# Order of a step's VectorE work in the attention: the next tile's maximum ahead of the older tile's mask

## The chip, the cores and the metric

One core of a Trainium2 chip runs the whole program in one launch. The metric is the device time of that core in microseconds (us). Engines are written as in the profile: PE is TensorE's matmul, PEld its weight load, DVE is VectorE, ACT ScalarE, POOL GpSimd, SP SyncE.

## The reference, cut to what matters

The program is a thresholded attention followed by two dense mixtures of experts. Only the attention is touched here.

```python
scores = scale * np.matmul(q, k.transpose(0, 1, 3, 2))        # batch 2, heads 8, 576 x 576, head size 64
thresh = np.max(scores, axis=-1, keepdims=True) - tau
scores = np.where(scores >= thresh, scores, -1000000000.0)
scores = scores - np.max(scores, axis=-1, keepdims=True)
attn = np.exp(scores)
attn = attn / (np.sum(attn, axis=-1, keepdims=True) + 1e-09)
return np.matmul(attn, v).astype(np.float32)
```

The result, 1152 tokens of 512 numbers, goes through eight experts with gates that are normalised eight times over rows and columns, and then through four experts with given weights. Each expert is `relu(x @ w1) @ w2` with 1024 hidden columns. All of it is float32; most products are made from a high and a low part of each operand.

## The kernel before, in words

The attention works on 72 tiles ("units") of 128 query rows by all 576 keys, one after the other, in a software pipeline that is written out by hand: the program order of each engine is the order of the code, and nothing moves an instruction afterwards. `Attention.step` (lines 389 to 429) issues one step. In step t it handles seven units at different ages; the names used here are those of line 394:

- `nxt` is unit t+2: PE makes its scores (`scores`, line 253) into a PSUM tile `sc`. There are two such tiles, so the scores of unit t+2 can't start before unit t's tile has been read for the last time.
- `a` is unit t+1: DVE takes the row maximum of its scores (`top`, line 275), then derives from it the bias of the exponential and the threshold (`line`, lines 279 and 280); ACT then takes the exponential (`exp`, line 284).
- `d` is unit t: DVE compares its scores with the threshold and multiplies the exponential by the result, with the row sum as a by-product (`mask`, line 288; this is the last reader of unit t's `sc`). Then come the sum's guard (`guard`, line 292) and the reciprocal (`norm`, line 296), and POOL scales the tile (line 298).
- `x` is unit t-2: PE transposes it into `et` (`turn`, lines 306 and 308); ACT copies it out as `eth` or `e` (`hi`, line 313); DVE forms the low part `etl` (`lo`, line 323).
- `c`, `z` and `y` are older units, which PE multiplies by the values (`mix`, lines 341, 348, 350), with outputs copied by ACT and DVE.

The pieces that DVE runs for `a` and `d`, and the exponential between them:

```python
def top(self, u):
    V.tensor_reduce(st[:, 0:1], u["sc"][:, :, :HS], axis=AX.XY, op=ALU.max)
def line(self, u):
    V.tensor_scalar(st[:, 1:2], st[:, 0:1], lin[:, 0:1], None, op0=ALU.mult)      # the bias
    V.tensor_scalar(st[:, 2:3], st[:, 0:1], lin[:, 1:2], None, op0=ALU.subtract)  # the threshold
def exp(self, u):
    A.activation(ex, u["sc"][:, :, :HS], AF.Exp, bias=u["st"][:, 1:2], scale=esc)
def mask(self, u):
    V.scalar_tensor_tensor(ex, u["sc"][:, :, :HS], st[:, 2:3], ex, op0=ALU.is_ge, op1=ALU.mult,
                           accum_out=st[:, 3:4])
def guard(self, u):
    V.tensor_scalar(u["st"][:, 4:5], u["st"][:, 3:4], 1e-9, None, op0=ALU.add)
def norm(self, u):
    V.reciprocal(st[:, 5:6], st[:, 4:5])                    # then POOL scales the tile
```

Within a step PE's program order is: the transposes of `x`, the older exact units' value products, `fill(0)`, the scores of `nxt`, the other value products, `fill(1)`. `fill` is expert work that has nothing to do with this tile: from step 20 on, up to three groups of 12 expert matmuls a step (lines 461 and 489) with their own ACT and DVE instructions (`hh` line 467, `hl` line 470). There is none in steps 0 to 19 and 36 to 39. Until the first expert runs, steps cut expert weights into high and low parts instead (ACT line 96, then POOL line 98 or, in even steps, DVE line 100). POOL's order within a step is: scale of `d`, the weights' low part, the low part of the next keys (`kl`, line 76) and of the next queries (`qs`, line 240). The first units' scores come straight from float32 operands (line 261), all others from split ones (line 270).

After step 76 the attention is over; the experts that are left run to the end.

Of the kernel before, what the change touches and what calls it, by code (L numbers as in the profile page):

```python
# [29 lines left out]
def attention_two_moe_kernel(ctx, tc, qP, kP, qT, kT, vp, tau, wg, w1, w1s, w2, dp, m2w1s, m2w2, out):  # L30
# [80 lines left out]
    class Attention:  # L111
# [277 lines left out]
        def step(self, fill, side):  # L389

            us, t = self.units, self.t
            un = lambda i: us[i] if 0 <= i < len(us) else None
            self.load()
            nxt, a, d, x, c, z, y = (un(t + i) for i in (2, 1, 0, -2, -3, -4, -5))
            if x:
                self.turn(x)
            if d:
                self.mask(d)
            if a:
                self.top(a)  # L400
            if d:
                self.guard(d)
            if a:
                self.line(a)
            if d:
                self.norm(d)
            for part, u in ((2, y), (1, z), (0, c)):
                for g in u["mix"] if u else ():
                    if g["head"]["exact"]:
                        self.mix(g, part)  # L410
            if x:
                self.hi(x)
            for u, late in ((z, False), (y, True)):
                for g in u["mix"] if u else ():
                    if late == (g["head"]["exact"] and g["head"]["h"] < H - 1):
                        self.out(g)
            fill(0, bool(c and c["mix"]))
            if a:
                self.exp(a)
            if x:  # L420
                self.lo(x)
            if nxt:
                self.scores(nxt)
            self.run(self.later)
            for g in c["mix"] if c else ():
                if not g["head"]["exact"]:
                    self.mix(g, 0)
            fill(1, bool(c and c["mix"] or z and z["mix"]))
            self.run(self.late)
            for w in self.work.pop(t, ()):  # L430
                w()
            side()
            self.t += 1
            return self.t < len(us) + 5
# [74 lines left out]
    with ExitStack() as att:  # L509
# [23 lines left out]
        def side():  # L533
            if at.t >= -1:
                fetch(2)
            if at.t >= nA0 - 3 and raws and room[0] and (at.t < nA1 or room[0] > 2 or at.t % 2):
                room[0] -= 1
                cook()
            if at.t == 20:
                nc.sync.dma_start(wg_sb, wg)  # L540
                nc.sync.dma_start(dp_sb, dp)
            if at.t == 24:
                split(V, V, wg2[:, :, :E1], wg2[:, :, E1:], wg_sb)
# [26 lines left out]
        def fill(phase, busy):  # L570
            if phase == 0:
                if 0 <= at.t < nA0 - 3:
                    room[0] -= 1
                    cook(None if at.t % 2 else at.later)
                spent[0] = pull(3)
            elif left[0] or not busy:
                pull(max((RA1 if at.t < nA1 + 3 else RA2) - spent[0], 0), True)
# [502 lines left out]
```

## Time and profile before

| what | value |
|---|---|
| device time, median of 3 runs (lowest to highest) | 1357.63 us (1355.26 to 1357.83) |
| the profiled execution: span from first to last instruction | 1353.7 us |
| PE busy over the span | 1320.6 us (98%) |
| PEld busy | 1181.8 us (87%) |
| DVE busy | 679.6 us (50%) |
| ACT busy | 562.3 us (42%) |
| POOL busy | 688.6 us (51%) |
| first and last mask of the attention start at | 7.93 us and 238.46 us |

The profile gives for the profiled execution its span; what lies around the span is not in it. The median of the runs is 3.9 us above the span. Shares over the whole span say little here, because the attention is its first sixth and the other five sixths are expert matmuls; the prediction reads the attention by stages.

### The profile page before, as it was taken

What the parts mean: (1) busy time and instruction counts of PE and PEld (TensorE: products, weight loads), DVE (VectorE), ACT (ScalarE), POOL (GpSimd) and SP (SyncE); (2) the same over time, 40 slices, a digit from 0 to 9 for tenths busy, and PEclk for the clock granted to TensorE, in tenths of its full rate; (3) what the DMA queues carried; (4) which work ended last, traced back from release to release, by engine and by line L of the source; (5) the groups of instructions that cost most, each with busy time, mean ns of one, the idle gap of its engine ahead of it and who ended that gap; (6) DMA issues with size and microseconds to landing.
All of it is one profiled execution on the core that took longest, in us unless ns stands there. A gap on an engine that the chain in (4) does not pass through costs nothing.

```text
span 1353.7 us, 21670 instructions
## 1 busy us (share of the span) xinstructions
PE 1320.6 (98%) x8089; PEld 1181.8 (87%) x8089; DVE 679.6 (50%) x1600; ACT 562.3 (42%) x1291; POOL 688.6 (51%) x830
## 2 busy tenths in 40 slices
PE   7998999999999999999999999999899999999998
PEld 4588999899888989899898989989789889898987
DVE  6899999365853433434343343434433434343343
ACT  6877777322542423323242332325433334242331
POOL 5866976441774345345434533544963554354330
PEclk9999999999999999999999999999999999999999
DMA  5522330100221111111011111101111101110001
GB/s 173 173 85 72 93 96 26 32 24 24 91 66 39 55 47 40 48 40 62 24 55 47 40 48 40 63 24 56 37 34 55 48 24 56 47 60 27 32 8 63
DMA packets 42058, 73.63 MB, mean 54 GB/s; under 512 B 5088, under 2 KB 10336, under 8 KB 41952
## 3 DMA queue, kind: packets, MB, share of 16 engines
q1 hardware_dynamic: 41664, 71.96, 16.8%
q8 instruction: 64, 1.05, 0.3%
q14 instruction: 42, 0.34, 0.1%
q10 hardware_dynamic: 288, 0.28, 0.1%
HBM read 69.86 MB, written 2.36 MB: 53 GB/s over the span
## 4 chain that ended last, share of the span: by engine, by line
PE 83%; DVE 8%; POOL 4%; ACT 3%; issue 2%; DMA 1%; POOLq 0%; ACTq 0%; DVEq 0%
PE mm L997 37%; PE mm L887 32%; PE mm L489 5%; PE mm L461 3%; DVE ex L288 2%; DVE st L275 1%; PE sc L270 1%; PE et L306 1%; ACT ex L284 1%; PE pv L350 1%; PE pv L341 1%; PE pv L348 1%; POOL wl L76 1%; DVE etl L323 1%; DVE xy L772 0%
## 5 line engine op out<-in xcount | busy, mean ns | idle before, releaser
L997 PE MATMUL mm<-wh,hs 128*128 128x512 f32 x1344 | 436.7, 398 | 3.7 <-DVE hs L863 3.7
L76 POOL TENSOR_TENSOR wl<-raw,wh 128x512 fp32r<-128x512 f32 x154 | 199.1, 1304 | 328.4 <-ACT wh L71 326.5
L997 PEld LDWEIGHTS mm<-wh,hs 128*128 128x128 f32 x1344 | 253.0, 188 | 66.3 <-DVE hs L863 10.1
L1005 DVE SCALAR_TENSOR_TENSOR acc<-mm,p,acc 128x512 f32<-128x512 f32 x181 | 135.9, 751 | 308.1 <-PE mm L997 308.1
L997 PE MATMUL mm<-wl,hs 128*128 128x512 f32 x672 | 264.7, 394 | 0.0
L892 ACT COPY s<-mm 128x288 f32<-128x288 f32 x84 | 33.6, 401 | 453.5 <-PE mm L887 453.5
L863 DVE SCALAR_TENSOR_TENSOR hs<-mm,hs 128x288 fp32r<-128x288 f32 x252 | 114.8, 456 | 104.0 <-ACT hs L862 103.7
L997 PEld LDWEIGHTS mm<-wl,hs 128*128 128x128 f32 x672 | 127.0, 189 | 27.3
L887 PE MATMUL mm<-xh,wl 128*128 128x288 f32 x672 | 144.3, 296 | 2.6 <-ACT w L892 1.4
L887 PE MATMUL mm<-xl,wh 128*128 128x288 f32 x672 | 143.8, 295 | 0.0
L887 PE MATMUL mm<-xh,wh 128*128 128x288 f32 x672 | 143.8, 295 | 0.0
L862 ACT ACTIVATE hs<-mm 128x288 fp32r<-128x288 f32 x252 | 104.2, 414 | 71.8 <-DVE mm L914 66.6
L76 POOL TENSOR_TENSOR wl<-ws,wh 128x512 fp32r<-128x512 f32 x88 | 114.5, 1305 | 36.6 <-ACT wh L71 26.9
L887 PEld LDWEIGHTS mm<-xh,wl 128*128 128x128 f32 x672 | 110.0, 188 | 7.3 <-ACT w L892 1.9
L887 PEld LDWEIGHTS mm<-xh,wh 128*128 128x128 f32 x672 | 108.1, 188 | 0.0
L887 PE MATMUL mm<-xth,wl 128*128 128x288 f32 x504 | 107.9, 295 | 0.0
L887 PEld LDWEIGHTS mm<-xl,wh 128*128 128x128 f32 x672 | 107.9, 188 | 0.0
L887 PE MATMUL mm<-xth,wh 128*128 128x288 f32 x504 | 107.7, 295 | 0.0
L887 PE MATMUL mm<-xtl,wh 128*128 128x288 f32 x504 | 107.7, 295 | 0.0
L869 POOL TENSOR_SCALAR ht<-hs 128x128 fp32r<-128x128 f32 x168 | 49.2, 298 | 112.9 <-ACT hs L862 97.8
L71 ACT CAST wh<-raw 128x512 fp32r<-128x512 f32 x154 | 95.7, 624 | 13.3 <-PE mm L887 10.4
L625 POOL TENSOR_TENSOR ws<-raw 128x512 f32<-128x512 f32 x44 | 57.7, 1311 | 54.6 <-DMA raw<-in_w1s 32.5
(169 smaller groups left out, 2412.0 us busy)
## 6 DMA issues: line engine op xcount, KB each, us to landing
raw<-in_w SPq DMA_DIRECT2D x88, 256.0 KB, 3.0
raw<-in_w1s SPq DMA_DIRECT2D x56, 256.0 KB, 2.8
raw<-in_m2w1s SPq DMA_DIRECT2D x32, 256.0 KB, 2.7
raw<-in_m2w SPq DMA_DIRECT2D x32, 256.0 KB, 2.8
kr<-in_kT SPq DMA_DIRECT2D x22, 288.0 KB, 2.9
vr<-in_vp SPq DMA_DIRECT2D x24, 160.0 KB, 2.3
qr<-in_qT SPq DMA_DIRECT2D x8, 288.0 KB, 2.8
out_y<-acc SPq DMA_DIRECT2D x8, 256.0 KB, 2.0
```

Of the source, the lines that this page charges most:

```text
L71: A.copy(hi, src)
L76: el.tensor_tensor(lo, src, f(hi), op=ALU.subtract)
L461: T.matmul(ph[:, :n], lhsT=a[:, kt * P:(kt + 1) * P], rhs=x[:, kt, n0:n0 + n], start=i == 0 and kt == 0, stop=i == 2 and kt == KT - 1)
L489: T.matmul(py[:, :256], lhsT=x, rhs=a[:, c0:c0 + 256], start=i == 0, stop=i == 3 * FT - 1)
L625: G.tensor_tensor(s, a, b, op=op)
L862: A.activation(hh, src, AF.Relu)
L863: V.scalar_tensor_tensor(hl, src, 0.0, f(hh), op0=ALU.max, op1=ALU.subtract)
L869: G.tensor_scalar(tail[j][:, :, q:q + 32], f(side[s][j][:, :, 2 * P:]), 1.0, 1.0, op0=ALU.mult, op1=ALU.mult)
L887: T.matmul(m, lhsT=w[:, (2 * g + kt) * P:(2 * g + kt + 1) * P], rhs=operand(u, kt, lo), start=first and j == 0, stop=j == len(ops) - 1, sk ...
L892: A.copy(z[name], m)
L997: T.matmul(py, lhsT=hs[x][:, k, o:o + P], rhs=w, start=n == 0, stop=n == 3 * HF - 1)
L1005: V.scalar_tensor_tensor(acc[t], py, s, acc[t], op0=ALU.mult, op1=ALU.add)
```

## The change

In each step DVE took the mask of unit t, the maximum of unit t+1, the guard of t, bias and threshold of t+1, the reciprocal of t. Now it takes the maximum of t+1, the mask of t, bias and threshold of t+1, then guard and reciprocal of t next to each other. No instruction is added or removed, and no other engine's order is changed.

```diff
             if x:
                 self.turn(x)
+            if a:
+                self.top(a)
             if d:
                 self.mask(d)
             if a:
-                self.top(a)
+                self.line(a)
             if d:
                 self.guard(d)
-            if a:
-                self.line(a)
-            if d:
                 self.norm(d)
```

One step of DVE in the middle of the attention, before; `etl`, `eth` and `xf` are the step's other DVE work, and the bracket names the engine whose semaphore an instruction waits for:

```order
L288 SCALAR_TENSOR_TENSOR ex,st<-sc,st,ex 128x576 [waits DVE_49,Activation_49]
L275 TENSOR_REDUCE st<-sc 128x1 [waits PE_49]
L292 TENSOR_SCALAR st<-st 128x1 [waits DVE_49]
L279 TENSOR_SCALAR st<-st,lin 128x1 [waits DVE_49]
L280 TENSOR_SCALAR st<-st,lin 128x1
L296 RECIPROCAL st<-st 128x1 [waits DVE_49]
L323 TENSOR_TENSOR etl<-et,eth 128x4x128 [waits Activation_49]
```

The same step now:

```order
L275 TENSOR_REDUCE st<-sc 128x1 [waits PE_49]
L288 SCALAR_TENSOR_TENSOR ex,st<-sc,st,ex 128x576 [waits Activation_49]
L279 TENSOR_SCALAR st<-st,lin 128x1 [waits DVE_49]
L280 TENSOR_SCALAR st<-st,lin 128x1
L292 TENSOR_SCALAR st<-st 128x1 [waits DVE_49]
L296 RECIPROCAL st<-st 128x1 [waits DVE_49]
L323 TENSOR_TENSOR etl<-et,eth 128x4x128 [waits Activation_49]
```

The maximum, which waits for PE, now stands ahead of the mask, which waits for ACT; the reciprocal follows directly on the guard, whose result it reads.

The start of the attention on PE (the scores of the first four units in float32, then the first transposes and the first split scores), which is the same before and now:

```order
L261 MATMUL sc<-kr,qr 128x288 [waits DMAHW1_49,DMAHW0_49]
L261 MATMUL sc<-kr,qr 128x288 [waits DMAHW5_49]
L261 MATMUL sc<-kr,qr 128x288 x2
L261 MATMUL sc<-kr,qr 128x288 [waits DVE_49,PE_49]
L261 MATMUL sc<-kr,qr 128x288
L261 MATMUL sc<-kr,qr 128x288 [waits DVE_49,PE_49]
L261 MATMUL sc<-kr,qr 128x288
L306 MATMUL et<-ident,ex 128x128 [waits Pool_49]
L306 MATMUL et<-ident,ex 128x128 x3
L308 MATMUL er<-ident,ex 64x128
L270 MATMUL sc<-kh,qs 128x288 [waits DVE_49,PE_49,Pool_49]
```

From the third unit on, each unit's scores wait for DVE, namely for the mask that frees their `sc` tile. PE's row is unchanged; the DVE instruction that it waits for has moved one place back.

## Rows read from the trace of the kernel before

**Rows 1.** Stages: stretch, length; busy PE, PEld, DVE, ACT, POOL; clock, DMA.

```profile
122.00:141.00 19.00, 15.09 (x104) 13.16 (x103) 17.59 (x52) 13.04 (x24) 12.09 (x18) 1.00 0.19 58
141.00:240.00 99.00, 96.93 (x763) 94.48 (x762) 92.20 (x283) 75.48 (x148) 74.84 (x104) 1.00 0.23 72
```

**Rows 2.** The chain that ended last, around 40 us: start, length, engine and line.

```profile
39.10 0.84 ACT ex L284
...
39.96 0.82 DVE ex L288 x2
```

**Rows 3.** The same chain from 62 to 240 us, shares by line.

```profile
by line: PE mm L489 13.7%; PE mm L461 10.2%; DVE ex L288 7.9%; PE sc L270 7.7%; DVE st L275 6.8%; PE et L306 6.7%; issue 6.4%; PE pv L350 4.9%; PE pv L348 4.3%; ACT ex L284 3.8%; DVE etl L323 3.1%; POOL ex L298 2.0%; PE pv L341 2.0%; DVE st
```

**Rows 4.** DVE's waits, 6 to 240 us: total us, times, longest.

```profile
DVE ex L288 <- ACT ex L284: 15.0, 31, 1.7
```

**Rows 5.** The same wait, 62 to 240 us.

```profile
DVE ex L288 <- ACT ex L284: 5.8, 19, 0.8
```

**Rows 6.** PE at the start: start, length, operation [idle before, releaser].

```profile
3.49 4.35 PE L261 MATMUL sc<-kr,qr 64*128 64x288 f32 x8 [3.49 <-DMA qr<-in_qP]
8.91 2.25 PE L261 MATMUL sc<-kr,qr 64*128 64x288 f32 x4 [1.06 <-DVE ex L288]
...
15.51 0.85 PE L270 MATMUL sc<-kh,qs 128*128 128x288 f32 x2 [0.39 <-POOL qs L240]
16.16 0.68 PE L270 MATMUL sc<-kl,qs 128*128 128x288 f32 x2
...
23.06 0.54 PE L270 MATMUL sc<-kh,qs 128*128 128x288 f32 x2 [2.38 <-POOL qs L240]
```

**Rows 7.** DVE at the start, one row of its timeline: the first mask.

```profile
7.93 0.82 DVE L288 SCALAR_TENSOR_TENSOR ex<-sc,st,ex 128x576 f32<-128x576 f32 x1 [0.84 <-ACT ex L284]
```

**Rows 8.** POOL at the start, one row of its timeline: unit 3 is scaled.

```profile
18.85 0.74 POOL L298 TENSOR_SCALAR ex<-ex,st 128x576 f32<-128x576 f32 x1 [2.55 <-DVE st L296]
```

**Rows 9.** DVE's timeline over one even step without expert work.

```profile
39.96 0.82 DVE L288 SCALAR_TENSOR_TENSOR ex<-sc,st,ex 128x576 f32<-128x576 f32 x1 [0.77 <-ACT ex L284]
...
40.70 0.75 DVE L275 TENSOR_REDUCE st<-sc 128x1 f32<-128x576 f32 x1
...
41.49 0.21 DVE L279 TENSOR_SCALAR st<-st,lin 128x1 f32<-128x1 f32 x1
...
41.74 0.15 DVE L296 RECIPROCAL st<-st 128x1 f32<-128x1 f32 x1
...
42.14 1.14 DVE L100 TENSOR_TENSOR wl<-raw,wh 128x512 fp32r<-128x512 f32 x1
43.20 0.81 DVE L288 SCALAR_TENSOR_TENSOR ex<-sc,st,ex 128x576 f32<-128x576 f32 x1
```

**Rows 10.** PE's timeline, the scores of three steps running.

```profile
38.14 0.53 PE L270 MATMUL sc<-kh,qs 128*128 128x288 f32 x2 [0.56 <-DVE ex L288]
...
41.13 0.53 PE L270 MATMUL sc<-kh,qs 128*128 128x288 f32 x2
...
44.07 0.40 PE L270 MATMUL sc<-kh,qs 128*128 128x288 f32 x1 [0.59 <-DVE ex L288]
```

**Rows 11.** First of 18 close pairs: a mask, and the scores behind it.

```profile
67.34 0.80 DVE L288 SCALAR_TENSOR_TENSOR ex<-sc,st,ex 128x576 f32<-128x576 f32 x1
...
68.29 0.37 PE L270 MATMUL sc<-kh,qs 128*128 128x288 f32 x1 [0.32 <-DVE ex L288]
```

**Rows 12.** Last of the 18 close pairs.

```profile
220.18 0.82 DVE L288 SCALAR_TENSOR_TENSOR ex<-sc,st,ex 128x576 f32<-128x576 f32 x1
...
221.56 0.30 PE L270 MATMUL sc<-kh,qz 128*128 128x288 f32 x1
```

**Rows 13.** PE's longest wait in total, 62 to 240 us.

```profile
PE et L306 <- DVE etl L323: 6.3, 9, 1.0
```

**Rows 14.** DVE before the attention: an instruction, and one reading its result.

```profile
4.39 0.15 DVE L527 TENSOR_SCALAR on<-tau_sb 128x1 f32<-128x1 f32 x1 [2.58 <-DMA tau_sb<-in_tau]
4.58 0.15 DVE L528 TENSOR_SCALAR esc<-on 128x1 f32<-128x1 f32 x1
```

## The prediction

> **What bounds the kernel now.** I read the busy times by stage first, then the chain that ended last, then the waits, then the timelines of DVE and PE side by side. The stages show that the attention has no single bound. From 141 to 240 us PE is busy 97 of 99 us, its weight loads 94 and DVE 92; in the stretch without expert work, 122 to 141 us, DVE is busy 17.6 of 19 us and PE only 15.1 [rows 1]. So DVE and PE are both nearly full and hand work to each other in every step. The reader is to see in the chain at 40 us a ring on which no engine is full: the exponential of unit t+1 on ACT (0.84 us) releases its mask on DVE, after the mask come the next maximum, guard and bias, and the bias releases the next exponential [rows 2]. One turn takes 0.86 us (39.10 to 39.96) for the exponential, 0.74 us from mask to maximum, 0.79 us from there to the bias (of it 0.12 for the guard's place, so 0.67 for the maximum), and 0.3 us from the bias to the exponential (estimated): 2.7 us. While the exponential runs, DVE stands still for 0.77 us [rows 9]. DVE waits so 31 times in the attention, 15.0 us in all [rows 4], and 19 of these times, 5.8 us, lie behind 62 us [rows 5]. The maximum could run in these gaps, and that is what the new order does.
>
> What it costs is on PE. There are two score tiles; the mask is the last reader of one, and PE can start scores 0.87 us after the start of the mask that frees their tile (43.20 to 44.07) [rows 9, 10]. The new order puts 0.67 us of maximum ahead of the mask, and the maximum itself waits for PE. So a ring that did not bind before can: scores, maximum, mask, scores.
>
> **The change, part by part.** No instruction is added or removed, and PE, ACT, POOL and SP keep their orders, so no DMA moves on its queue. Four things change.
>
> *1. The start.* The first scores are slow: units 0 and 1 end at 7.84 us (3.49 + 4.35), and unit 2 takes 2.25 us [rows 6]. Before, the first mask started at 7.93 and the scores of unit 2 followed 0.98 us later [rows 6, 7]. Now the maximum of unit 1 goes first, from 7.9 us; the mask follows at 8.55, scores 2 run from 9.5 to 11.8, maximum 2 follows, mask 1 at 12.5, scores 3 from 13.4 to 15.7, maximum 3, mask 2 at 16.4, scores 4 at 17.3 instead of 15.51, 1.33 us long (15.51 to 16.84), maximum 4 at 18.6, mask 3 at 19.3. Its reciprocal comes 1.2 us behind it (0.74 for the mask, 0.12 to 0.13 for each of two small instructions, 0.19 for the guard), and POOL can scale unit 3 at 20.7 us. Before it did so at 18.85 us, after 2.55 us of waiting for this reciprocal [rows 8]; behind it on POOL stand the weights', keys' and queries' low parts, for which PE waits at 23.06 us [rows 6]. All of that moves by 1.9 us. Bounds: 0, if other work covers it, and 3.
>
> *2. The steps without expert work, 32 to 50 us.* Two steps take 5.93 us (38.14 to 44.07) [rows 10]. The new ring for two steps: scores 0.8 (two pairs of matmuls of 0.53, which overlap), maximum 0.67, mask to reciprocal 1.18, from there through the other DVE work to the next step 1.46 (41.74 to 43.20), maximum 0.67, mask to scores 0.87 [rows 9, 10]; together 5.65 us. That is 0.28 less, three times: 0.8 us gained. Behind 50 us PE runs without a gap up to the expert work, and nothing is gained. Parts 1 and 2 give +1.1 us.
>
> *3. The steps with expert work, and 36 to 39.* I set each mask's start against that of the scores it releases. If DVE did not wait for the exponential, the mask moves by 0.67 us, and the scores can't start before 0.67 + 0.87 = 1.54 us behind the old start of the mask. From step 19 on, 18 pairs are closer than that, the first with 0.95 us [rows 11], the last with 1.38 [rows 12]; what is missing, less what DVE waited anyway, sums to 6.5 us. Not all of it is lost: nine times, 6.3 us in all, PE waits at its next transposes for DVE's `etl` [rows 13], and a late score matmul can vanish there. But PE's later end moves the transposes, ACT's copy and DVE's `etl` with it, and that has hardly any slack. I take half, 3.3 us; the ends are 0 and 6.5. Against it stands the gain from DVE's waits. On the chain between 62 and 240 us the mask has 7.9% of 178 us, or 14 us, which is 17 masks of 0.82 us out of 53 [rows 3]. A third of the 5.8 us of waits [rows 5] is thus on the path: 1.9 us gained; the ends are 0 and 5.8.
>
> *4. Guard and reciprocal side by side.* The reciprocal now waits for the instruction just ahead of it. Such a pair of small instructions starts 0.19 us apart (4.39 and 4.58) [rows 14]; in the old order two steps of the small work take 0.25 us (41.49 to 41.74), so about 0.12 each [rows 9]. That is 0.07 us a step. It counts where DVE is on the chain, in the same 17 steps: 1.2 us. The ends are 0 and 72 x 0.07 = 5.0 us. The Trainium skill (VectorE: DVE Perf Modes, "The DRAIN you can't avoid") says that chaining VectorE instructions with or without semaphores takes the same time. By that rule this part would be nothing and the forecast 1.2 us lower; the 0.19 us above speaks against it for small instructions.
>
> Sum: 1.1 + 3.3 - 1.9 + 1.2 = +3.7 us. Against the profiled execution's span of 1353.7 us that gives 1357.4 us; the median of the runs is 3.9 us above that span, which I take over: **1361.3 us**. What follows the attention is mostly PE's expert work, so I let the whole shift through.
>
> **The rivals.**
>
> *Faster: the exponential's ring decides.* If PE's close pairs vanish in its waits for `etl` and the start is covered, what is left is the gain: 0.8 us of part 2 and up to all 5.8 us of waits, less 1.2 us for the reciprocal: -5.4 us, 1352.2 us. For it: the wait recurs 31 times, and on the chain at 40 us it is what ends last [rows 2, 4]. Against it: behind 62 us the chain runs through PE for longer than through the mask, and PE has 2 us of idle time in 99 [rows 1, 3]. It decides where DVE, not PE, ends a step in more than the 17 of 53 steps. The Trainium skill's advice (Perfetto Trace Analysis, "Optimization Strategy") is to find the recurring gaps on the engine that should be full and to make what they wait for start sooner; by it this rival would be the forecast. Chance 0.2.
>
> *No change: the slack takes both.* PE's expert matmuls fill what the new order moves, the start's delay is swallowed by the later queue on POOL, and the sum stays within 0.2%, 2.7 us, which is about what a measurement of this kernel can tell from no change: 1357.6 us. For it: PE and DVE are both near full, so neither can be moved far. Chance 0.24.
>
> *Much slower: every step pays.* All close pairs count in full and every step pays the reciprocal: 1.1 + 6.5 + 5.0 = +12.6 us, 1370.2 us. It decides if PE is bound to the mask at every step. Chance 0.1, within slower.
>
> That the change does not do what it says I leave out: DVE's rows stand in the new order, and nothing reorders them.
>
> **How the numbers follow.** The forecast and the much slower case have 0.56 together, faster 0.2, no change 0.24. The range leaves out the outer part of the faster rival and the last of the much slower one: 1354.0 to 1368.5 us.
>
> **What would show it.** Right, step by step: the masks' waits for the exponential fall from 15.0 us to a few; the maximum gets a wait for PE's scores, which it hardly had, above all before 30 us; the scores of unit 6 start near 25 us instead of 23.06; two steps near 40 us take about 5.65 us; PE's waits for the mask grow behind 62 us; the last mask starts about 4 us later than at 238.46 us; guard and reciprocal stand 0.19 us apart. Wrong: the last mask earlier than before, or the start unmoved, or PE's waits for the mask unchanged while the time rises.

## The result and the profile after

The changed kernel takes **1364.38 us** (median of four runs; 1363.16 to 1366.98), the kernel before beside it 1357.63 us (median of three; a fourth run, of 2225.16 us, is far out of line and counts nowhere). The ratio on record is 1.0065, 95% interval 1.0052 to 1.0078: **8.8 us slower** (7.1 to 10.6). That is inside the range and on the side of the forecast, but 5 us more than its +3.7 us. The medians of these few runs stand only 6.7 us apart, which the ratio does not rest on alone. The clock speaks for the larger figure: three of the four changed runs had a mean granted clock of 0.997 and took 1363.16 to 1364.47 us, while 28 runs of the kernel before at 0.997, in the experiments below, have a median of 1355.8 us, some 8.5 us less.

The profiled execution took 1364.47 us, with a span of 1362.7 us against 1353.7 us: +9.0 us. In every run of the experiments the time is 1.7 to 1.9 us above the span. So the profiled execution of the kernel before took about 1355.5 us, a quick one, and of the 3.9 us that the prediction added to its span some 2 us are the difference between two runs; its shift of +3.7 us does not hang on that.

Where it arises is read from the masks, the same instruction in both traces. The table gives how much later than before it starts.

| place | later than before, us | added in between, us |
|---|---|---|
| first scores on PE (their load landed later) | 0.24 | 0.24 |
| mask of unit 8 | 2.95 | 2.71 |
| mask of unit 19 | 4.27 | 1.32 |
| last mask, unit 71 | 7.67 | 3.40 |
| gate's first maximum (line 717; 718 before) | 7.44 | -0.23 |
| gate's first normalisation (line 730; 731 before) | 8.91 | 1.47 |

Behind the gate nothing more is added. The three stretches of the attention are taken one by one below.

The busy times by stage in the changed kernel, with the columns of [rows 1]:

```profile
122.00:141.00 19.00, 14.11 (x105) 12.85 (x104) 17.01 (x53) 12.35 (x24) 10.21 (x13) 1.00 0.23 64
141.00:240.00 99.00, 95.50 (x737) 92.39 (x738) 92.17 (x275) 75.98 (x148) 77.42 (x109) 1.00 0.25 73
```

Against [rows 1], PE is 1.4 us less busy in the last stage and 1.0 us less in the one ahead of it, while DVE does in the last as much as before. The windows are the same in both, so the changed kernel is 6 to 8 us less far in them. No work was added; PE waits more. What DVE waits for between 6 and 240 us, in the changed kernel (total, times, longest):

```profile
DVE st L275 <- PE sc L270: 9.9, 18, 2.0
DVE etl L323 <- ACT eth L313: 5.0, 12, 1.0
DVE st L275 <- PE sc L261: 4.8, 4, 1.9
```

The wait of [rows 4], mask for exponential, 15.0 us in 31 places, is gone from the list. The maximum now waits for PE's scores instead: 9.9 + 4.8 = 14.7 us in 22 places, where it waited 0.8 us in one place before. Behind 62 us it is 3.3 us of these, and the wait for ACT's `eth` has gone from 2.7 to 5.0 us. Taken together the gap was not filled, it changed its name. What PE waits for between 62 and 240 us:

```profile
PE et L306 <- DVE etl L323: 4.7, 9, 0.9
PE sc L270 <- DVE st L279: 4.2, 5, 1.6
PE sc L270 <- DVE ex L288: 1.5, 3, 1.2
```

The wait of [rows 13] has shrunk from 6.3 to 4.7 us, as PE comes later to it. The scores' wait for the mask has grown to 4.2 + 1.5 = 5.7 us, from 2.0 us in the same view of the kernel before:

```profile
PE sc L270 <- DVE ex L288: 2.0, 3, 1.0
```

The profile names the bias of line 279, which stands right behind the mask, for part of it. In the chain that ended last, from 62 to 240 us, the shares by line, to be held against [rows 3]:

```profile
by line: PE sc L270 14.2%; PE mm L488 13.8%; PE mm L460 9.2%; PE et L306 8.0%; DVE ex L288 7.7%; PE pv L350 7.3%; DVE st L275 7.1%; PE pv L348 6.0%; DVE etl L323 4.7%; issue 2.6%; DVE eth L326 2.5%; DVE hl L469 2.5%; PE pv L341 2.0%; PE er 
```

The scores have nearly doubled their share, 7.7 to 14.2%, and ACT's exponential has left these first places: the ring now closes over PE. The timelines show it in each stretch. DVE in the changed kernel, the start, then two steps at 40 us, then the mask of the first close pair, then the gate:

```profile
8.14 0.76 DVE L275 TENSOR_REDUCE st<-sc 128x1 f32<-128x576 f32 x1 [0.80 <-PE sc L261]
...
27.09 0.76 DVE L275 TENSOR_REDUCE st<-sc 128x1 f32<-128x576 f32 x1 [2.00 <-PE sc L270]
27.77 0.81 DVE L288 SCALAR_TENSOR_TENSOR ex<-sc,st,ex 128x576 f32<-128x576 f32 x1
...
40.58 0.81 DVE L288 SCALAR_TENSOR_TENSOR ex<-sc,st,ex 128x576 f32<-128x576 f32 x1
...
41.56 0.14 DVE L292 TENSOR_SCALAR st<-st 128x1 f32<-128x1 f32 x1
41.74 0.16 DVE L296 RECIPROCAL st<-st 128x1 f32<-128x1 f32 x1
42.29 0.76 DVE L275 TENSOR_REDUCE st<-sc 128x1 f32<-128x576 f32 x1 [0.38 <-PE sc L270]
42.96 0.81 DVE L288 SCALAR_TENSOR_TENSOR ex<-sc,st,ex 128x576 f32<-128x576 f32 x1
...
46.58 0.80 DVE L288 SCALAR_TENSOR_TENSOR ex<-sc,st,ex 128x576 f32<-128x576 f32 x1
...
71.61 0.80 DVE L288 SCALAR_TENSOR_TENSOR ex<-sc,st,ex 128x576 f32<-128x576 f32 x1
...
282.41 0.28 DVE L721 TENSOR_REDUCE gm<-mm 1x1 f32<-1x128 f32 x1 [3.82 <-PE mm L720]
```

PE in the same places: the scores of units 2, 3 and 6, of a step at 41 us, and those behind the first close pair's mask:

```profile
9.78 2.25 PE L261 MATMUL sc<-kr,qr 64*128 64x288 f32 x4 [1.67 <-DVE st L279]
13.71 2.26 PE L261 MATMUL sc<-kr,qr 64*128 64x288 f32 x4 [1.68 <-DVE st L279]
...
25.73 0.85 PE L270 MATMUL sc<-kh,qs 128*128 128x288 f32 x2 [1.76 <-POOL qs L240]
...
41.46 0.53 PE L270 MATMUL sc<-kh,qs 128*128 128x288 f32 x2 [0.77 <-DVE ex L288]
...
72.57 0.50 PE L270 MATMUL sc<-kh,qs 128*128 128x288 f32 x2 [0.98 <-DVE st L279]
```

And POOL's scaling of unit 3, which [rows 8] had at 18.85 us:

```profile
21.07 0.74 POOL L298 TENSOR_SCALAR ex<-ex,st 128x576 f32<-128x576 f32 x1 [1.65 <-DVE st L296]
```

In the kernel before, the scores of unit 3 on PE and mask 5 on DVE stood here:

```profile
11.61 2.25 PE L261 MATMUL sc<-kr,qr 64*128 64x288 f32 x4 [0.45 <-DVE ex L288]
```

```profile
23.48 0.81 DVE L288 SCALAR_TENSOR_TENSOR ex<-sc,st,ex 128x576 f32<-128x576 f32 x1
```

*Start.* PE waits 1.67 and 1.68 us where it waited 1.06 [rows 6] and 0.45: one turn of scores, maximum and mask takes 3.93 us (9.78 to 13.71), before 2.70 (8.91 to 11.61). POOL comes to unit 3 2.2 us later, and the scores of unit 6 start at 25.73 instead of 23.06. Then comes something that the prediction did not have: mask 5 stands behind the maximum of those scores (27.09 to 27.77), where before it ran at 23.48 without them. PE's clock has a part in the 2.71 us of the table as well: the pair at 25.73 still takes 0.85 us, where the one at 23.06 took 0.54 [rows 6]. In the five experiments below that leave the steps up to 7 as they were, mask 8 comes 0.04 to 0.94 us late by such differences alone, so one profile can't size the start to better than about 1 us.

*Around 40 us.* Two steps take 6.00 us (40.58 to 46.58), not 5.65; [rows 9, 10] had 5.93. One step did become shorter, 2.38 us from mask to mask (40.58 to 42.96), before 2.70, as the exponential no longer ends it, but there the maximum waits 0.38 us for PE. The other became longer, 3.62 us, before 3.24. The chain that ended last shows what sets the two together (changed kernel, start, length, engine and line):

```profile
40.67 0.74 DVE ex L288 x2
...
41.46 0.80 PE sc L270 x4
...
42.80 0.59 PE pv L341 x2
...
43.47 0.54 ACT e L313
...
44.25 0.63 ACT wh L96
...
44.90 1.09 DVE wl L100
...
46.66 0.74 DVE ex L288 x2
```

From one mask the chain goes over PE's scores, transposes and value products to ACT's copy `e`, to the weights' high part `wh` that stands behind it on ACT, to the weights' low part `wl` on DVE, and over the maximum to the mask after next.

*Behind 62 us.* The scores of the first close pair start 0.96 us behind their mask, as in [rows 11] (0.95). But that mask is now 4.27 us later than in [rows 11], 3.71 of them inherited from mask 18; the rest is most of the 0.67 us of maximum ahead of it, and PE waits 0.98 us where it waited 0.32.

*At the gate.* The wait of line 721 is 3.82 us, and PE's clock shows why. The windows' row of the changed kernel for 278 to 281 us (PE, PEld, DVE, ACT, POOL busy; granted clock; DMA):

```profile
278.00:281.00 3.00, 3.00 (x17) 3.00 (x16) 0.59 (x2) 0.00 (x0) 0.00 (x0) 0.53 0.04 16
```

The same work in the kernel before, 270 to 273 us:

```profile
270.00:273.00 3.00, 3.00 (x26) 2.98 (x26) 0.59 (x2) 0.22 (x1) 0.00 (x0) 1.00 0.14 54
```

PE is full in both, but at 0.53, which is mostly the level of 1.2 GHz, it ends 17 matmuls where it ended 26 at 2.4 GHz. Just ahead, PE ran a group of 18 very small matmuls, and 0.5 us behind its end the clock fell:

```profile
275.54 2.17 PE L714 MATMUL mm<-both,lt 16*128 16x8 f32 x18
```

The kernel before runs the same group at 268.10 us, and its clock stays at 1.00. The kernel before waits there, in its own DVE timeline, 1.5 us less:

```profile
273.50 0.28 DVE L722 TENSOR_REDUCE gm<-mm 1x1 f32<-1x128 f32 x1 [2.34 <-PE mm L721]
```

### The profile page after: what moved, and what is told of

Same layout as the page of the kernel before. It is cut to its first block, busy times and chain, and to the rows that moved or that the text cites. A ratio compares the mean times of both kernels' runs of the same rounds, so it can differ in the third digit from the quotient of the medians.

```text
span 1362.7 us, 21601 instructions
## 1 busy us (share of the span) xinstructions
PE 1324.4 (97%) x8089; PEld 1184.5 (87%) x8089; DVE 681.9 (50%) x1600; ACT 562.2 (41%) x1291; POOL 688.9 (51%) x830
## 4 chain that ended last, share of the span: by engine, by line
PE 86%; DVE 7%; POOL 3%; ACT 2%; issue 1%; DMA 0%; POOLq 0%; ACTq 0%; DVEq 0%
PE mm L996 37%; PE mm L886 32%; PE mm L488 5%; PE mm L460 4%; PE sc L270 2%; DVE ex L288 1%; PE et L306 1%; DVE st L275 1%; PE pv L350 1%; PE pv L348 1%; PE pv L341 1%; DVE etl L323 1%; PE sc L261 1%; POOL wl L76 1%; DVE xy L771 0%
```

## The experiments

Theory: the loss is the maximum that PE's scores must be finished for and that now stands ahead of the mask that PE waits for. It costs at the start, a little without expert work, and behind step 19 in the close pairs. Rivals: the pair of guard and reciprocal carries it; the start does not reach the end; all of it is the clock. Each kernel is run against the kernel before on the same chip, five rounds each. Differences in us are the ratio less 1, times 1357. Beside them stand the masks of the profile, which show where it arises. A third figure is the difference *at equal clock*. The runs of one kernel are not all granted the same mean clock: over the 96 runs of the kernel before, 0.001 of it goes with 1.1 us (the medians are 1358.6 us at 0.995 and 1354.3 us at 0.999). A straight-line fit to the runs that the ratios use (a level for each chip, a step for each kernel, one slope for the clock) takes this out. It is an estimate, good to 0.4 to 0.6 us, and it takes out a stretch at 1.2 GHz whether the edit brought it or not. In all experiments the instructions are the same; only DVE's order differs.

### Parts of the change by kind

**The pair: guard moved next to the reciprocal, mask still ahead of the maximum.**

```diff
             if a:
                 self.top(a)
-            if d:
-                self.guard(d)
             if a:
                 self.line(a)
             if d:
+                self.guard(d)
                 self.norm(d)
```

> The old order with one difference: the guard is moved down to stand directly before the reciprocal (mask, maximum, bias, threshold, guard, reciprocal). Theory, the score ring: the loss comes from the maximum standing ahead of the mask, and the adjacent pair costs 0.06 us a step only where DVE is on the path, so +0.3 to +1.3 us over before. Rival, the adjacent pair: each of 72 steps pays 0.06 us, +4 to +5 us, half of the change's loss.

Measured: ratio 1.0036 (1.0024 to 1.0048), +4.9 us (at equal clock +4.2). That is the rival's number, but this is no pure test of the pair. The guard had also stood between the maximum and the bias that reads it. DVE in this kernel, one step:

```profile
38.27 0.82 DVE L288 SCALAR_TENSOR_TENSOR ex<-sc,st,ex 128x576 f32<-128x576 f32 x1
...
39.01 0.75 DVE L275 TENSOR_REDUCE st<-sc 128x1 f32<-128x576 f32 x1
39.80 0.21 DVE L279 TENSOR_SCALAR st<-st,lin 128x1 f32<-128x1 f32 x1
...
40.05 0.14 DVE L292 TENSOR_SCALAR st<-st 128x1 f32<-128x1 f32 x1
40.23 0.16 DVE L296 RECIPROCAL st<-st 128x1 f32<-128x1 f32 x1
```

The bias starts 0.79 us after the maximum; in [rows 9] it did so too, but with the guard inside that time. From mask to reciprocal it is now 40.23 - 38.27 = 1.96 us, before 1.78 (39.96 to 41.74): 0.18 a step, of which 0.06 is the pair. The masks are 0.83 us late at unit 7, with the clock of the start in it, and 4.84 at the last: the 4.0 us between are as many as 22 steps of 0.18, a third of the 64. That fits the prediction's third of the steps that DVE ends (17 of 53); it does not show it. For the pair's own price the next kernel is the better one, since the changed kernel has a mask between maximum and bias.

**The maximum ahead of the mask, small instructions kept apart** (bias, guard, threshold, reciprocal; `cut` is the threshold's line taken out of `line`).

```diff
+            if a:
+                self.top(a)
             if d:
                 self.mask(d)
             if a:
-                self.top(a)
+                self.line(a)
             if d:
                 self.guard(d)
             if a:
-                self.line(a)
+                self.cut(a)
             if d:
                 self.norm(d)
```

> The maximum ahead of the mask as in the change, but the guard stands between bias and threshold, so that no small instruction follows directly on the one whose result it reads (maximum, mask, bias, guard, threshold, reciprocal). Theory, the score ring: nearly the whole loss stays, +7 to +9 us over before. Rival, the adjacent pair: half of it goes, +3.5 to +5 us over before.

Measured: ratio 1.0043 (1.0029 to 1.0057), +5.8 us, between the two expectations; at equal clock +7.8, for its five runs were granted 0.9984 on average and those of the kernel before 0.9966. The last masks of the changed kernel and of this one, in that order:

```profile
246.13 0.82 DVE L288 SCALAR_TENSOR_TENSOR ex<-sc,st,ex 128x576 f32<-128x576 f32 x1
```

```profile
245.11 0.82 DVE L291 SCALAR_TENSOR_TENSOR ex<-sc,st,ex 128x576 f32<-128x576 f32 x1
```

1.02 us is what the pair costs in the changed kernel, by these two profiles. The other 6.65 us come with the maximum's place (clock of the start included): the rival that the pair carries the loss falls.

**Only the 18 steps with close pairs** (that order if `t` is one of 19, 21, 23, 25, 26, 28, 36 to 39, 43, 47, 55, 56, 58, 61, 63, 65).

```diff
+            if t in (19, 21, 23, 25, 26, 28, 36, 37, 38, 39, 43, 47, 55, 56, 58, 61, 63, 65):
+                ...
+            else:
+                ...
```

> Only the maximum goes ahead of the mask, and only in the 18 steps of the prediction's close pairs (mask to scores under 1.54 us from step 19 on); the small instructions keep the spacing of the order before, so the pair of guard and reciprocal costs nothing here. If the close pairs are what makes the change slow behind step 19 (the prediction's part 3): last mask +3.3 us (0 to 6.5), 1360.7 us. Rival, DVE decides there and PE's late scores vanish in its waits for the transposed weights: last mask within 1 us of before, 1357.4 us. A third: the pairs cost, but the exponential's waits that go give it back in the same steps, below +1 us.

Measured: ratio 1.0018 (1.0007 to 1.0029), +2.4 us (at equal clock +3.5). In the profile the masks move from 0.95 us late at step 18 (a longer stretch at 1.2 GHz in the start, where nothing is edited) to 5.00 us at the last: +4.05 us in the attention. PE's waits, 62 to 240 us, in this kernel:

```profile
PE et L309 <- DVE etl L326: 4.4, 8, 0.9
PE sc L270 <- DVE st L279: 4.3, 5, 1.6
PE sc L270 <- DVE ex L291: 1.4, 2, 1.2
```

These are nearly the changed kernel's, from 18 edited steps. The close pairs make PE's waits for the mask, and cost 2.4 (time) to 4.05 us (masks). The time has an advantage that is not the edit's: its runs were granted a mean clock of 0.9972, those of before beside them 0.9962. The two rivals, nothing and below 1 us, fall.

**Only the other 35 steps from 19 on** (the same edit with `t > 18` and not one of those 18).

> The counterpart of the run on the close pairs: the maximum ahead of the mask in the other 35 steps from step 19 on, the order before in the 18 close pairs and up to step 18. By the prediction the masks' waits for the exponential that are on the path are gained here and no pair costs anything: last mask -1.9 us, 1355.5 us. Rival, these waits only change their name (the maximum waits for PE's scores, or PE for the transposed weights): within 0.7 us of before. The profile of the picked steps speaks for the rival in 8 of its 14 steps, and for a gain of 0.2 to 0.9 us at steps 4, 30 and 60.

Measured: ratio 0.9986 (0.9975 to 0.9997), **-1.9 us**: faster, as forecast. At equal clock it is -0.8 us. By the masks it is -0.8 us too: the last is 1.30 us late, less 0.6 us in the start and 1.5 us for a stretch at 1.2 GHz at 131 us that the kernel before does not show. 1.5 us is what such a stretch costs there in the three kernels whose steps 36 to 43 are unedited (steps up to 7, up to 2, and the 14 picked ones). DVE's waits, 62 to 240 us, in this kernel:

```profile
DVE etl L326 <- ACT eth L316: 6.1, 11, 1.5
DVE st L275 <- PE sc L270: 2.2, 7, 0.4
DVE ex L291 <- ACT ex L287: 1.8, 5, 0.8
```

Of the 5.8 us of [rows 5], 1.8 are left, in unedited steps. But 2.2 us of waits for the scores have come, and the wait for ACT's `eth`, 2.7 us before, is 6.1, of which 1.5 us follows the stretch. So most of the waits change their name here too, as the rival says; what is left of the gain shows in the masks and the time, and it is a smaller one than the 4.0 us of waits that went. The reorder does gain where PE is not waiting for the mask.

**Both groups, all steps from 19 on.**

> The maximum ahead of the mask in all steps from step 19 on, close pairs and others together, the small instructions at the spacing of before. If the two groups add up (+2.4 and -1.9 us by their times), this gives +0.5 us, 1358.2 us, and what the late steps of the change lose beyond it (+4.9 in all) is the pair of guard and reciprocal. If the pair costs only the 1.0 us that the last masks of the changed kernel and of the one without the pair stand apart, this run gives about +3.5 to 3.9 us, 1361.4 us: then neighbouring steps take from each other what they gain alone.

Measured: ratio 1.0032 (1.0022 to 1.0043), +4.3 us; masks from 0.95 to 4.35 us late, +3.4 us. By the masks the groups add up (4.05 - 0.8 = 3.25). By the times they don't (+0.5 against +4.3), and the clock is most of that gap: at equal clock it is 3.5 - 0.8 = 2.7 against 3.8. This kernel's profile has a stretch at 1.2 GHz at the gate, 274 to 278 us, of 1.5 us, which those of the two groups alone do not have. The 1.1 us that remain lie within the three errors added up.

### Parts of the change by place

All four have the change's own order, guard and reciprocal side by side, in the steps named, and the order before in the others:

```diff
+            if t < 8:
+                ...
+            else:
+                ...
```

**Steps up to 7.**

> The change's order in steps below 8 alone, the old order from step 8 on. Theory, the score ring: the start's delay of 3.0 us (the mask of step 8 came 2.95 us later in the change's profile) goes through to the end, +2.5 to +3.5 us over before. Rival, the start is swallowed by PE's later work: 0 to +1 us, and the change's loss must then come from the later steps alone.

Measured: ratio 1.0018 (1.0008 to 1.0028), +2.4 us; at equal clock +3.9, as its runs were granted 0.9982 and those of before 0.9966. From mask 8 to mask 39 every mask is 3.3 to 3.5 us late, with no way back; at 134 us a stretch at 1.2 GHz adds 1.5. About 1 us of it is PE's clock in the start: at 29.66 us a pair of this kernel's scores still takes 0.85 us, before 0.53 at 29.96. What is lost at the start reaches the end: that rival falls.

**Steps up to 2.**

> The change's order in steps 0 to 2 alone, where the maximum waits for scores of 2.25 us. By the prediction's part 1 the whole delay of the start is made here and goes through POOL: POOL scales unit 3 about 2 us later than at 18.85, PE gets the queries' low part of unit 6 that much later, masks from 8 on +1.9 us, 1358.6 us. If the delay is made by masks 3 to 7 that now stand behind a maximum, this run gives below +1 us, for the waits of POOL and of the masks (1.68 us at step 6) swallow it. If POOL's chain decides and nothing swallows it, it gives the +3 to 3.9 us of the whole start, 1360.0 us.

Measured: ratio 1.0020 (1.0010 to 1.0030), +2.7 us (at equal clock +2.4). The masks of units 3, 4 and 5 on DVE, before at 16.82, 19.86 and 23.48 us, come in this kernel at 18.68, 21.73 and 25.34 us; the last of them:

```profile
25.34 0.81 DVE L291 SCALAR_TENSOR_TENSOR ex<-sc,st,ex 128x576 f32<-128x576 f32 x1
```

Each is 1.86 or 1.87 us late, 0.17 of it because the first load landed later, and POOL scales unit 3 at 20.71 us, 1.86 late: part 1, nearly to the tenth. Behind that the masks go to +3.2, for here PE stays at 1.2 GHz until 31 us, as the windows' row of 27 to 31 us shows (clock 0.50):

```profile
27.00:31.00 4.00, 4.00 (x14) 2.58 (x13) 1.80 (x8) 2.77 (x5) 3.33 (x5) 0.50 0.72 220
```

**Steps 3 to 7.**

> The change's order in steps 3 to 7 alone. By the prediction nothing is lost here: 0, or the -0.3 to -0.9 us that step 4 gained alone. By the changed kernel's trace mask 5 stands behind maximum 6, which waits for scores that wait for POOL: before, it started at 23.48 us, and those scores ended at 24.07; with the maximum (0.67 us) ahead the mask cannot start before 24.8: +1.3 us at mask 5, and +0.5 to +1.5 us from mask 8 on, as the wait of 1.68 us at mask 6 takes some of it. Rival: swallowed, within 0.5 us of before at mask 8. With the run on steps 0 to 2 it should add to the +3.9 us that the start alone gave at equal clock.

Measured: ratio 1.0011 (1.0000 to 1.0021), +1.5 us (at equal clock +2.2). Maximum 6 and mask 5 on DVE in this kernel:

```profile
25.25 0.76 DVE L275 TENSOR_REDUCE st<-sc 128x1 f32<-128x576 f32 x1 [2.00 <-PE sc L270]
25.92 0.81 DVE L291 SCALAR_TENSOR_TENSOR ex<-sc,st,ex 128x576 f32<-128x576 f32 x1
```

Mask 5 is 2.4 us late, since it stands behind the maximum; mask 9 still 0.8, 0.25 of it there from the first mask on. That leaves 0.6 us, with the start's clock in it. This is the part of the start that the prediction did not have. With steps 0 to 2 it gives 2.7 + 1.5 = 4.2 us by the times, against 2.4 (1.1 to 3.8) in one, and 2.4 + 2.2 = 4.6 at equal clock, against 3.9; by the masks 1.7 + 0.6 = 2.3, beside 2.7 in the changed kernel.

**Steps 8 to 18.**

> The change's order in steps 8 to 18 alone, the order before elsewhere. By the prediction (two steps take 5.65 us instead of 5.93): last mask -0.8 us, 1356.6 us. By the trace of the changed kernel (a ring through PE's transposes, ACT's high parts and DVE's low parts, two steps 6.0 to 6.1 us): +0.5 to +0.8 us, 1358.1 us. Neither can be told from no change by the time alone; the masks 8 to 19 in the profile tell them apart.

Measured: ratio 1.0005 (0.9996 to 1.0013), not to be told from no change by the time. In the profile mask 8 is 0.04 us late, mask 19 1.01, and every one from there to the last 1.0 to 1.1: +1.0 us (at equal clock +1.0 too), a loss, where a gain of 0.8 was forecast.

**Steps from 19 on.**

> The change's order from step 19 on alone, with guard and reciprocal side by side. By the prediction's part 3 and 4: +3.3 - 1.9 + 1.2 = +2.6 us, 1360.0 us. By the changed kernel's trace from mask 19 to the last: +3.4 us, 1360.8 us. If the three stretches add up (start +2.4 by the times, 8 to 18 +0.8, this one +3.4), they give 6.6 of the 8.8 us and 2 us are left to stretches of half clock at the gate. If this run alone gives +5 or more, the late steps carry the change and the start does not reach the end.

Measured: ratio 1.0036 (1.0022 to 1.0050), +4.9 us (at equal clock +4.2); masks from 0.17 to 5.73 late, of which a stretch at 1.2 GHz at 133 us makes about 1.4 (against the masks of the run of both groups, this kernel's stand 0.3 us earlier ahead of it and 1.1 us later behind it), so +4.1 us. With the start's 2.4 and 0.7 for steps 8 to 18, the three parts give 8.0 of the 8.8 us; at equal clock 3.9 + 1.0 + 4.2 = 9.1 us. So the rival that all of it is the clock falls too.

### Versions meant to be faster

**Maximum first in 14 picked steps** (4, 8, 10, 12, 14, 16, 18, 30, 32, 34, 50, 55, 60, 68: where the mask waited for the exponential and no scores stood close behind it).

> The maximum ahead of the mask in 14 steps alone (4, 8, 10, 12, 14, 16, 18, 30, 32, 34, 50, 55, 60, 68): those in which, in the profile of before, the mask waited at least 0.3 us for its exponential and the next scores were ready before that wait or within 0.3 us of its start. All other steps keep the old order. Theory, the score ring: in these steps the maximum fits into the wait and delays no mask, so the gain of the idea stays and its price goes: -2 to -4 us against before. Rival, any step with the maximum first costs its share of the loss: 14 of 72 steps, +1 to +2 us.

Measured: ratio 0.9984 (0.9974 to 0.9993), **-2.2 us**, 1355.01 us (median): it beats both kernels. At equal clock it is -1.1 us. By the masks, those of units 6 and 7 come 0.6 and 0.9 us earlier. That is PE's clock and not step 4: the mask right behind the edit, unit 5's, is not earlier at all, and the same four value products take 1.08 us here and, in the stretch at 1.2 GHz, 1.97 us before, in this order:

```profile
24.44 1.08 PE L344 MATMUL pv<-e,vr 128*64 128x256 f32 x4
```

```profile
25.06 1.97 PE L341 MATMUL pv<-e,vr 128*64 128x256 f32 x4
```

Steps 30 and 60 give 0.2 to 0.3 us each. Steps 8 to 12 and 32, 34, 50, 55, 68 give nothing, for a later wait takes it back, and the 0.6 us that steps 14 and 16 give are lost again at step 18. At the last mask that is -1.4 us, when two stretches at 1.2 GHz (1.0 and 1.5 us) that the kernel before does not show are taken off its +1.12, and some 0.5 to 0.6 us without the 0.9 of the start's clock.

**Step 4 and the 35 other steps from 19 on.**

> A version that should beat both kernels: the maximum ahead of the mask in the 35 steps from 19 on that are no close pairs, and in step 4, where the mask waits 1.11 us for the exponential and no scores wait for the mask; the order before in all others. If the gains add up, -1.9 - 0.9 = -2.8 us, 1354.9 us. If step 4's gain is swallowed on the way, -1.9 us as without it. Rival, the gain behind step 19 was a chance of the half-clock stretches: within 0.7 us of before.

Measured: ratio 0.9993 (0.9983 to 1.0003), -0.9 us, not to be told from no change by the time; at equal clock -0.9 us too. The gains do not add up, since step 4 has none: masks 6 and 7 are 0.5 and 1.5 us late here, with a longer stretch at 1.2 GHz there, and in the run of both groups, whose start is unedited and as slow, they are 0.3 and 0.9 us late. From mask 18 to the last this profile and that of the 35 steps alone move by the same 0.69 us, each with a stretch at 131 us in it, so the gain of the 35 steps has come twice. Whether more is to be had this way is open: this version and the picked one differ by less than their intervals.

## Why the prediction was right or wrong

| step of the prediction | forecast | masks of the profiles | by the times | at equal clock (estimate) |
|---|---|---|---|---|
| 1, the start | +1.9 | +2.7; alone, steps 0 to 2 +1.7, steps 3 to 7 +0.6 | +2.4 (1.1 to 3.8) | +3.9; alone, +2.4 and +2.2 |
| 2, steps 8 to 18 | -0.8 | +1.0 to 1.3 | +0.7 (-0.5 to 1.8) | +1.0 |
| 3, close pairs | +3.3 | +4.05 | +2.4 (1.0 to 3.9) | +3.5 |
| 3, gain from DVE's waits | -1.9 | -0.8 | -1.9 (-3.4 to -0.4) | -0.8 |
| 4, guard and reciprocal | +1.2 | +1.0 | +3.0, from two ratios whose intervals overlap | +0.4 from step 19 on, within the errors |
| none, stretch at the gate | 0 | +1.5 | not apart | taken out |

**The size: about half.** The forecast was +3.7 us, the ratio gives 8.8. The terms missed in one direction, all towards slower: the start by 0.8 us (masks) to 2.0 (equal clock), steps 8 to 18 by 1.8 to 2.1, the gain by 1.1, and the stretch at the gate was not in the sum. That the time still lies inside the range is owed to the range's width.

**Bound and mechanism: right.** The ring of scores, maximum, mask, scores binds where the prediction said, at the start and in the close pairs, and PE's waits for the mask grew as its last paragraph asked for. The sign held for that reason: with the start and the close pairs left out the same reorder is faster.

**Part 1: right in its chain, short at its end.** Masks 1 to 3 were forecast at 12.5, 16.4 and 19.3 us and came at 12.74, 16.68 and 19.65, 0.24 of it the later load. The step that failed is "all of that moves by 1.9 us". It followed POOL's queue to PE's scores of unit 6 and stopped; in the new order a late score is also a late mask, through the maximum, and steps 3 to 7 paid 0.6 us for it by the masks, 1.5 (0 to 2.8) by the time and 2.2 at equal clock.

**Part 2: wrong sign.** The step that failed is "together 5.65 us". The ring that I summed had PE's scores right behind the mask and nothing else of PE's. The trace after shows two steps in 6.00 us. The step that the exponential ended did go down, 2.70 to 2.38 us, but the wait moved: PE's scores end later, and so do its transposes and value products, ACT's copies and high parts, and DVE's low parts ahead of the next maximum. That this second ring sets the 6.00 us is read from the chain that ended last, which goes once round it from mask to mask (40.67 to 46.66); no run took one of its links away.

**Part 3: both signs right, the gain too large.** The pairs were set at half of 6.5 us; masks give 4.05, equal clock 3.5 and the time 2.4. The gain was set at a third of the 5.8 us. The time met it (-1.9), but part of that is clock and so luck: masks and equal clock give 0.8, as most of the waits came back under another name. In sum -1.9 + 3.3 = +1.4 was forecast, and the run of both groups gave +3.4 us by its masks.

**Part 4: right.** 0.17 to 0.18 us from guard to reciprocal in the changed kernel (0.19 was assumed), and 1.0 us at the last mask. The Trainium skill (VectorE: DVE Perf Modes, "The DRAIN you can't avoid") reports eight copies with a semaphore after each as no slower than with one after the last, so that the semaphore costs nothing extra. For these 128x1 instructions, where the second reads what the first wrote, the trace disagrees: 0.18 us against the 0.12 us between neighbours that don't wait for each other.

**Not foreseen: the stretch at the gate**, 1.5 us. It is in the profiles of the four kernels that have the maximum first in every step from 19 on (the changed one among them), and in none of the other ten. All 14 profiles run the group of 18 small matmuls there; in the four the clock falls between 0.1 us ahead of its end and 1.1 us behind it, in the ten it does not fall. With one profile each I can't say that the reorder causes it, and what decides it stays open.

**The rivals.** "The exponential's ring decides" was true only in the far steps, by 0.8 to 1.9 us, and not the 5.8 us that it needed. "Much slower" had the price of all close pairs in full; they cost 2.4 to 4.05 of 6.5. "No change" failed since nothing of the start was swallowed on the way: with the start alone changed, mask 39 is as late as mask 9 (3.5 us).

A third score tile would take the mask out of PE's way altogether. It was not tried: the eight PSUM banks are all in use.

## What to carry to other kernels

A wait that recurs 31 times is worth filling only with work that is itself ready then: ask of the piece that is pulled forward what it waits for, and of the piece that is pushed back who waits for it. Here the second answer was a double-buffered PSUM tile's last reader, and 15.0 us of one wait became 14.7 us of another. Deciding it step by step (pull forward only where no one stands close behind the mask) turned a loss of 8.8 us into a gain of 2.2 us by the time (0.9 to 3.5), of which about half is the clock that those runs were granted.

## What the hardware showed that was not expected

- **Stretches at 1.2 GHz in a kernel whose PE is 98% busy.** Each profile has one to four ahead of its last 3 us, in places that differ between profiles of nearly equal kernels: 22 to 31, 69 to 73, 131 to 138, 274 to 282, 378 to 391 us. PE is nearly full in them, but not ahead of them: of the 28 stretches the 24 that are not at the gate follow closely on idle time of PE, 1.3 to 2.4 us of it, as the wait of 2.38 us ahead of 23.06 us in [rows 6]. Not every such gap is followed by one: that of 1.58 us ahead of 241.96 us in the kernel before is not. Where PE is on the path a stretch moves the masks by 1.0 to 1.5 us. They go with most of the spread between runs of one kernel: of 96 runs of the kernel before, those with a mean granted clock of 0.995 have a median of 1358.6 us, those with 0.999 1354.3 us. A difference of 2 us between two profiles means nothing until the clock of both is read stretch by stretch.
- **The clock's record is not whole at the start.** In the kernel before, the scores at 15.51 us take 0.85 us for a pair [rows 6] and at 38.14 us 0.53 us [rows 10], while the clock reads 1.00 in both places. In one profile (both groups from step 19 on) a pair still takes 0.85 us at 27.29 us, with no stretch at 1.2 GHz listed before the gate; only the durations tell it.
- **A small DVE instruction that reads its neighbour's result** starts 0.17 to 0.18 us after it instead of 0.12, and a bias that reads the maximum of 128x576 directly ahead of it 0.79 us instead of 0.67 us after it. One independent instruction in between hides either. Leaving them together in all steps cost 0.18 us in the step shown, and in all 4.0 us by the masks (4.9 by the time).
